# Gathered rows turned by VectorE in 32x32 blocks behind transfers inside SBUF, in place of TensorE transposes

## The chip, the cores and the metric

The kernel runs on one core of a Trainium2 chip. The metric is the device time of one execution in microseconds (us). Before the change the median of three executions was 1307.16 us (1306.89 to 1311.0); the profiled execution took 1307.46 us, of which 1305.5 us are the span that the trace covers. TensorE is PE in the profile, VectorE is DVE, ScalarE is ACT, GpSimd is POOL, SyncE is SP.

## What is computed

The input is an attention step over channels, followed by a layer of eight experts that choose their tokens by a sorted list.

```python
def _attn_ref(q, k, v, tau):                      # B, N, C = 4, 5056, 256
    qn = q / (np.linalg.norm(q, axis=1, keepdims=True) + 1e-06)
    kn = k / (np.linalg.norm(k, axis=1, keepdims=True) + 1e-06)
    s = kn.transpose(0, 2, 1) @ qn / tau
    a = np.exp(s - s.max(-1, keepdims=True))
    a /= a.sum(-1, keepdims=True) + 1e-09
    return v @ a                                  # x: 20224 tokens of 256

def _moe_ref(x, w_gate, w1, w2):                  # E, F = 8, 1024; cap = 2528
    order = np.argsort(-(x @ w_gate).flatten())
    # each token goes to the first expert in this order that still has room
    for e in range(E):
        mask = assigned == e
        out[mask] = np.maximum(x[mask] @ w1[e], 0.0) @ w2[e]
```

Every expert gets exactly 2528 tokens, that is 19 columns of 128 and one of 96 on a chip with 128 partitions.

## The kernel before, in words

**Stages.** To about 320 us the kernel computes the attention and writes its output x, row by row, to a table `x_d` in HBM. From there to the end it runs the experts one after another. Which tokens an expert gets is found while the expert ahead of it is computed: `route` and `compact` are generators whose steps are mixed into the work of the experts, most of them on VectorE, with small matmuls on TensorE (lines 585, 598, 794) and sums on ScalarE (line 851).

**Chunks.** An expert's 20 columns are cut in chunks: six in expert 0 (2, 4, 4, 4, 4, 2 columns) and five of four columns in the others. For every column `load_x` lets GpSimd gather 128 rows of `x_d` into `xg` (line 1088; two buffers), 256 numbers for each token. The matmuls need the rows turned, with the 256 numbers along the partitions. `turn` does that: for each half of the 256 (`kb`) and each column one PE transpose into a PSUM tile `ph` (line 1125), eight for a chunk of four columns; then ScalarE writes the high part `xH` (line 1131) and VectorE the rest `xL` (line 1134), because each product is computed as three products of a high and a low part.

**Layers.** `layer1` runs 8 blocks of 6 matmuls for a chunk (line 1162) into `ph`, four buffers that it shares with `turn`; ScalarE writes `hH` (line 1165), VectorE `hL` (line 1170). `layer2` runs 24 matmuls for each column into `py` (line 1194, two buffers); ScalarE copies the result to `y` (line 1199) and GpSimd scatters it to the output (line 1201). The order is layer1 of chunk c, then layer2 of chunk c-1. `turn` of chunk c+1 stands in layer2 of c-1 behind its first column, and asks for the gathers of the chunk two further on; `gather` then issues one of them behind each block or column (two for the first chunk of an expert). The first chunk of the next expert is turned in the last layer2 of an expert (`next_turn`), once its gathers are taken to have landed; its second one in the first layer1, at block 5.

**What sets the order.** The program writes the order of every engine out by hand. `Order` keeps two clocks, `o.pe` and `o.dve`, in estimated nanoseconds; `post` puts a VectorE step with a due time and a price into a line, `hook` runs the earliest of that line and of the routing steps, `flush` runs the line up to a tile. Each engine then executes its own instructions in the order written; they wait for each other by semaphores alone. The waits that the estimates stand for (`GATHER_LAT`, 7500) issue nothing.

Of the kernel before, what the change touches and what calls it, by code (L numbers as in the profile page):

```python
# [74 lines left out]
LAYER_LAT = 1050  # L75
SPLIT_LAT = 1600
LOAD_LAT = 8500
GATHER_LAT = 7500
START_TICKS = 27
EARLY_PRIO = 4  # L80
COMPACT_PRIO = 2
# [5 lines left out]
def attention_moe(ctx: ExitStack, tc: tile.TileContext, q, k, vt, tau, wg, w1t, w2t, tabs, out):  # L87
# [990 lines left out]
    def load_x(p, c, paced=False):  # L1078
        idx = routed[p]["src"]
        xg = ffx.tile([128, 4, C], F32, name="xg", bufs=2)  # L1080

        def fetch(i, col, n):
            at = idx[:n, col:col + 1]
            if paced:
                at = ffx.tile([128, 1], I32, name="pace", bufs=4)[:n]
                S.activation(at, idx[:n, col:col + 1], AF.Copy)
            P.memset(spacer, 0.0)
            P.indirect_dma_start(out=xg[:n, i, :], out_offset=None, in_=x_d,  # L1088
                                 in_offset=bass.IndirectOffsetOnAxis(ap=at, axis=0))
        for i, col in enumerate(cols_of(p, c)):  # L1090
            queue.append((p, c, lambda i=i, col=col, n=n_in(col): fetch(i, col, n)))
        xgs[p, c] = xg

# [3 lines left out]
                queue.pop(0)[2]()  # L1097

    queue = []
    unit = [0]  # L1100
    phs = []
    turned = [0]
# [9 lines left out]
    def turn(p, c):  # L1112
        while any(e[:2] == (p, c) for e in queue):
            gather()
        xg = xgs[p, c]
        nt = n_of(p, c)
        xH = ffx.tile([128, 2, 512], F32R, name="xH")
        xL = ffx.tile([128, 2, 512], F32R, name="xL")
        xts[p, c] = (xH, xL)
        pts = []  # L1120
        for kb in range(2):
            pt = ph_tile()
            for i, col in enumerate(cols_of(p, c)):
                n = n_in(col)
                PE.transpose(pt[:, i * 128:i * 128 + n].bitcast(F32R), xg[:n, i, kb * 128:(kb + 1) * 128].bitcast(F32R),  # L1125
                             identr[:n, :n])
            pts.append((kb, pt, unit[0]))
        o.pe += 440
        o.hook()
        for kb, pt, u in pts:  # L1130
            S.activation(xH[:, kb, 0:nt], pt[:, 0:nt], AF.Copy)  # L1131

            def low(kb=kb, pt=pt):
                V.tensor_tensor(xL[:, kb, 0:nt], pt[:, 0:nt], xH[:, kb, 0:nt].bitcast(F32), op=OP.subtract)  # L1134
            o.post(o.pe + TURN_LAT + (90 + nt) * kb, 90 + nt, low, u)
        turned[0] = unit[0]
        ahead = chunks.index((p, c)) + 2
        if ahead < len(chunks):
            p_, c_ = chunks[ahead]
            want(("idx", p_), lambda: load_x(p_, c_))  # L1140
# [68 lines left out]
    with tc.manual_schedule():  # L1209
# [60 lines left out]
        for p in range(E):  # L1270
# [3 lines left out]
            def turn_at(c):  # L1274
                return lambda: turn(p, c)

            turns = [] if last else [p + 1]

            def next_turn(force=False):
                if not turns:  # L1280
                    return
                if force:
                    o.until(("idx", p + 1))
                    settle()
                    while queue:
                        gather()
                    while o.pe < routed[p + 1]["time"] + GATHER_LAT:
                        o.tick(100)
                if done.get(("idx", p + 1)) and o.pe >= routed[p + 1]["time"] + GATHER_LAT:
                    turn(turns.pop(), 0)  # L1290

            if not last:
                want(("ei", p + 1), lambda p=p: load_w(p + 1))
# [5 lines left out]
                layer2(p, 0, h[0], {1: [turn_at(1)]})  # L1299
                h[1] = layer1(p, 1, {5: [turn_at(2)]})  # L1300
            else:
                h[0] = layer1(p, 0, {5: [turn_at(1)], **pieces})
            for c in range(1 if p else 2, nchunk):
                h[c] = layer1(p, c, {})
                ins = {}
# [9 lines left out]
                    ins = {min(1, cuts[p][c - 1] - 1): [w1]}  # L1315
                layer2(p, c - 1, h[c - 1], ins)
            layer2(p, nchunk - 1, h[nchunk - 1], {i: [next_turn] for i in range(1, 4)})
            while turns:
                next_turn(True)


# [61 lines left out]
```

## Time and profile before

| what | value |
| --- | --- |
| median of three executions | 1307.16 us |
| profiled execution | 1307.46 us |
| its span | 1305.5 us |
| PE busy | 1284.6 us, 98% |
| DVE busy | 795.4 us, 61% |
| ACT busy | 559.2 us, 43% |
| POOL busy | 378.3 us, 29% |
| PE transposes of gathered rows (line 1125) | 320 |
| gathers (line 1088) | 160 |

Busy time of PE is the time with a matmul in the array; matmuls overlap, so what a matmul costs is read from the distance between the starts of two that follow each other, not from its own duration. A row of the timeline or of the chain of waits starts with the start in us and the length in us. A row of the groups ends with busy us, mean ns of one instruction, and the idle time before them with what ended it. A row of stages holds busy us of each engine with the number of instructions, then the granted PE clock (1.00 is full), the share of the DMA engines and GB/s.

### The profile page before, as it was taken

To read this page: it belongs to the slowest core of one execution; us is meant where nothing else is said; L and a number is where in the kernel's file an instruction comes from. 1 tells how busy PE (TensorE), PEld (TensorE's weight loads), DVE (VectorE), ACT (ScalarE), POOL (GpSimd) and SP (SyncE) were. 2 spreads that over 40 slices of the span, in tenths; PEclk is the share of its full clock that TensorE was granted. 3 is DMA by queue.
4 is the path that set the end of the run, shared out by engine and by line. 5 is a ranking of instruction groups with operands and counts; after the bars stand their busy time and mean duration, and the time that the engine had idled before them with its cause. 6 is when DMAs were issued, how large, how long until landed. Compare 5 with 4: busy or idle time off the path is not lost.

```text
span 1305.5 us, 23749 instructions
## 1 busy us (share of the span) xinstructions
PE 1284.6 (98%) x9381; PEld 1151.9 (88%) x9381; DVE 795.4 (61%) x1973; ACT 559.2 (43%) x1249; POOL 378.3 (29%) x690
## 2 busy tenths in 40 slices
PE   7999999998999999999999999999999999999998
PEld 6879976997889988898899888988989998898998
DVE  6778695998778677768667767663343224334321
ACT  6547743565324344325335435335543234334321
POOL 1000000001522534333324433342342433334222
PEclk9989999999999999999999999999999999999999
DMA  8999874345202213112112211221131113111100
GB/s 298 337 399 387 296 273 157 141 164 190 73 24 86 66 40 105 53 43 104 47 35 77 78 40 37 73 84 34 46 116 36 56 46 109 45 41 56 36 29 32
DMA packets 42638, 143.18 MB, mean 110 GB/s; under 512 B 8224, under 2 KB 13216, under 8 KB 37920
## 3 DMA queue, kind: packets, MB, share of 16 engines
q0 software_dynamic: 17664, 58.22, 13.7%
q1 hardware_dynamic: 15328, 62.40, 13.2%
q10 hardware_dynamic: 9536, 21.06, 4.1%
q8 instruction: 73, 1.20, 0.4%
q14 instruction: 37, 0.30, 0.1%
HBM read 99.97 MB, written 41.68 MB: 109 GB/s over the span
## 4 chain that ended last, share of the span: by engine, by line
PE 86%; issue 5%; DVE 5%; POOL 2%; DMA 1%; ACT 1%; POOLq 0%; SPq 0%; DVEq 0%; ACTq 0%
PE ph L1162 32%; PE py L1194 31%; PE s L309 8%; PE px L258 8%; PE pc L585 3%; PE ph L1125 2%; POOL out_dram L1201 1%; PE px L413 1%; PE pi L794 1%; DVE acc_k L318 1%; DMA x_d<-xs 1%; DVE acc_q L318 1%; DVE ua L1064 1%; DVE yy L372 1%; DMA ua<-in_q_dram 1%
## 5 line engine op out<-in xcount | busy, mean ns | idle before, releaser
L1194 PE MATMUL py<-ua,hH 128*128 128x256 f32 (+1 forms) x2560 | 464.7, 282 | 0.0
L1162 PE MATMUL ph<-xH,ua 128*128 128x512 f32 (+3 forms) x1312 | 415.3, 391 | 0.3 <-ACT xH L1131 0.3
L1194 PEld LDWEIGHTS py<-ua,hH 128*128 128x128 f32 (+1 forms) x2560 | 391.8, 186 | 2.7 <-issue 0.2
L1170 DVE SCALAR_TENSOR_TENSOR hL<-ph,hH 128x512 fp32r<-128x512 f32 (+3 forms) x328 | 219.7, 671 | 231.9 <-ACT hH L1165 226.5
L1194 PE MATMUL py<-ua,hL 128*128 128x256 f32 (+1 forms) x1280 | 358.4, 280 | 0.0
L1201 POOL DMA_INDIRECT out_dram<-y,idx x160 | 160.9, 1005 | 519.3 <-ACT y L1199 471.9
L1165 ACT ACTIVATE hH<-ph 128x512 fp32r<-128x512 f32 (+3 forms) x328 | 191.1, 583 | 238.2 <-PE ph L1162 232.6
L1162 PEld LDWEIGHTS ph<-xH,ua 128*128 128x128 f32 x1312 | 244.2, 189 | 48.3 <-ACT xH L1131 0.4
L1162 PE MATMUL ph<-xL,ua 128*128 128x512 f32 (+3 forms) x656 | 256.0, 390 | 0.6 <-DVE xL L1134 0.6
L1194 PEld LDWEIGHTS py<-ua,hL 128*128 128x128 f32 (+1 forms) x1280 | 238.6, 186 | 0.0
L1199 ACT ACTIVATE y<-py 128x256 f32<-128x256 f32 (+1 forms) x160 | 61.5, 384 | 340.2 <-PE py L1194 281.9
L1088 POOL DMA_INDIRECT xg<-x_d,src x156 | 156.3, 1002 | 78.9 <-issue 33.6
L309 PE MATMUL s<-ua 128*128 128x256 f32 x640 | 146.9, 390 | 7.1 <-DMA ua<-in_q_dram 7.1
L309 PEld LDWEIGHTS s<-ua 128*128 128x128 f32 x640 | 124.3, 196 | 27.8 <-issue 6.7
L1162 PEld LDWEIGHTS ph<-xL,ua 128*128 128x128 f32 x656 | 124.2, 189 | 23.6 <-DVE xL L1134 0.7
L317 ACT ACTIVATE sq<-ua 128x1024 f32<-128x1024 f32 x72 | 75.1, 1054 | 42.2 <-DVE acc_k L318 14.3
L1134 DVE TENSOR_TENSOR xL<-ph,xH 128x512 fp32r<-128x512 f32 (+3 forms) x82 | 51.1, 665 | 56.1 <-ACT xH L1131 56.1
L261 ACT ACTIVATE xs<-px 128x512 f32<-128x512 f32 (+1 forms) x96 | 49.7, 527 | 52.0 <-PE px L258 50.7
L258 PE MATMUL px<-aH,vh 128*128 128x256 f32 (+1 forms) x216 | 62.8, 293 | 0.4 <-ACT aH L220 0.4
L851 ACT ACTIVATE junk<-pi,rhalf 128x160 bf16<-128x160 f32 x140 | 53.9, 391 | 18.7 <-PE pi L794 18.1
L258 PE MATMUL px<-aH,vl 128*128 128x256 f32 (+1 forms) x216 | 61.2, 284 | 0.0
L258 PE MATMUL px<-aL,vh 128*128 128x256 f32 (+1 forms) x216 | 61.1, 284 | 0.0
(291 smaller groups left out, 1321.6 us busy)
## 6 DMA issues: line engine op xcount, KB each, us to landing
x_d<-xs ACTq DMA_DIRECT2D x39, 512.0 KB, 2.8
ua<-in_k_dram SPq DMA_DIRECT2D x35, 512.0 KB, 6.2
ua<-in_q_dram SPq DMA_DIRECT2D x35, 512.0 KB, 7.2
vr<-in_vt_dram SPq DMA_DIRECT2D x14, 1024.0 KB, 9.7
ua<-in_vt_dram SPq DMA_DIRECT2D x4, 1024.0 KB, 4.9
out_dram<-y,idx POOLq DMA_INDIRECT x160, 2.4
xg<-x_d,src POOLq DMA_INDIRECT x156, 2.8
ub<-in_vt_dram SPq DMA_DIRECT2D x2, 1024.0 KB, 12.6
```

The costliest lines, as they stand in the source:

```text
L258: mm = PE.matmul(px[:, i * C:i * C + width], lhsT=l_, rhs=a_, start=(j == 0), stop=(j == len(terms) - 1))
L309: newest[0] = PE.matmul(sb[:, ib * C:(ib + 1) * C], lhsT=kt[:, t, ib * 128:(ib + 1) * 128], rhs=qt[:, t, :], start=(first and t == 0 and i ...
L317: S.activation(sq, t_, AF.Square)
L851: S.activation(junk, pi[:, i * W:i * W + COLS], AF.Sign, bias=rhalf[:, g0 + i:g0 + i + 1], scale=-1.0, accum_out=sgn[:, g0 + i:g0 + i + 1])
L1088: P.indirect_dma_start(out=xg[:n, i, :], out_offset=None, in_=x_d, in_offset=bass.IndirectOffsetOnAxis(ap=at, axis=0))
L1134: V.tensor_tensor(xL[:, kb, 0:nt], pt[:, 0:nt], xH[:, kb, 0:nt].bitcast(F32), op=OP.subtract)
L1162: PE.matmul(ph[:, 0:nt], lhsT=l[:, w], rhs=x_[:, kb, 0:nt], start=(i == 0), stop=(i == 5))
L1165: S.activation(hH[:, fb, 0:nt], ph[:, 0:nt], AF.Relu)
L1170: V.scalar_tensor_tensor(hL[:, fb, 0:nt], ph[:, 0:nt], 0.0, hH[:, fb, 0:nt].bitcast(F32), op0=OP.max, op1=OP.subtract)
L1194: PE.matmul(py[:n, 0:C], lhsT=l[:, fb, tk], rhs=w[:, d], start=(j == 0), stop=(j == 23))
L1199: S.activation(y[:n], py[:n, 0:C], AF.Copy)
L1201: sd = P.indirect_dma_start(out=out, out_offset=bass.IndirectOffsetOnAxis(ap=idx[:n, col:col + 1], axis=0), in_=y[:n], in_offset=None)
```

## The change

For all chunks but the first three of expert 0 (38 chunks, 150 columns) the PE transposes go. Behind the last gather of such a chunk, `exchange` issues 16 transfers on SP's queue, each from 32 partitions of `xg` to 32 partitions of a new tile `xq` (two buffers), 8 pieces of 32 numbers for each partition. They bring each 32x32 block to the partitions on which it ends. `turn` then posts two DVE transposes of 128x512, which turn all blocks in place and write the same PSUM tiles, with the ScalarE copy to `xH` behind each; the steps to `xL` follow. The second chunk of the next expert may now be turned in the last layer2 as well; where it isn't, it is turned in the first layer1 at block 2. What is taken as the time to landing counts from the last gather and its exchange (`LANDED_LAT`, 7500).

```diff
@@ -75,7 +75,9 @@
 LAYER_LAT = 1050
 SPLIT_LAT = 1600
 LOAD_LAT = 8500
-GATHER_LAT = 7500
+LANDED_LAT = 7500
+FIRST_BY_V = 3
+TURN_FB = 2
 START_TICKS = 27
 EARLY_PRIO = 4
 COMPACT_PRIO = 2
@@ -1078,6 +1080,20 @@
     def load_x(p, c, paced=False):
         idx = routed[p]["src"]
         xg = ffx.tile([128, 4, C], F32, name="xg", bufs=2)
+        cols = cols_of(p, c)
+        by_v = p > 0 or c >= FIRST_BY_V
+
+        def exchange():
+            back = chunks.index((p, c)) - 2
+            o.flush(turn_unit.get(chunks[back], 0))
+            xq = ffx.tile([128, 4, 8, 32], F32, name="xq", bufs=2)
+            xgs[p, c] = xq
+            parts = xg.rearrange("p i (k m) -> p (i k) m", k=2)
+            for g in range(4):
+                n = sum(n_in(col) > 32 * g for col in cols)
+                for j in range(4):
+                    nc.sync.dma_start(xq[32 * j:32 * j + 32, g, 0:2 * n],
+                                      parts[32 * g:32 * g + 32, 0:2 * n, 32 * j:32 * j + 32])
 
         def fetch(i, col, n):
             at = idx[:n, col:col + 1]
@@ -1087,7 +1103,11 @@
             P.memset(spacer, 0.0)
             P.indirect_dma_start(out=xg[:n, i, :], out_offset=None, in_=x_d,
                                  in_offset=bass.IndirectOffsetOnAxis(ap=at, axis=0))
-        for i, col in enumerate(cols_of(p, c)):
+            if i == len(cols) - 1:
+                if by_v:
+                    exchange()
+                landed[p, c] = o.pe + LANDED_LAT
+        for i, col in enumerate(cols):
             queue.append((p, c, lambda i=i, col=col, n=n_in(col): fetch(i, col, n)))
         xgs[p, c] = xg
 
@@ -1097,6 +1117,8 @@
                 queue.pop(0)[2]()
 
     queue = []
+    landed = {}
+    turn_unit = {}
     unit = [0]
     phs = []
     turned = [0]
@@ -1118,16 +1140,40 @@
         xL = ffx.tile([128, 2, 512], F32R, name="xL")
         xts[p, c] = (xH, xL)
         pts = []
-        for kb in range(2):
+        by_v = p > 0 or c >= FIRST_BY_V
+        src = xg
+        for kb in range(2) if by_v else ():
+            pt = ph_tile()
+            u = unit[0]
+            pts.append((pt, u))
+
+            def turn_v(kb=kb, pt=pt):
+                rows = xg.rearrange("p g (i k) a -> p k i g a", k=2)[:, kb]
+                turned_ = pt.rearrange("p (i g n) -> p i g n", i=4, g=4)
+                full = nt // 128
+                V.transpose(turned_[:, 0:full], rows[:, 0:full])
+                if nt % 128:
+                    V.transpose(turned_[:, full, 0:nt % 128 // 32], rows[:, full, 0:nt % 128 // 32])
+                S.activation(xH[:, kb, 0:nt], pt[:, 0:nt], AF.Copy)
+            o.post(o.pe, 130 + nt * 1.13, turn_v, pts[0][1])
+        for kb, (pt, u) in enumerate(pts):
+            def low_v(kb=kb, pt=pt):
+                V.tensor_tensor(xL[:, kb, 0:nt], pt[:, 0:nt], xH[:, kb, 0:nt].bitcast(F32), op=OP.subtract)
+            o.post(o.pe + 1400 + 650 * kb, 90 + nt, low_v, u)
+            turn_unit[p, c] = u
+        for kb in () if by_v else range(2):
             pt = ph_tile()
             for i, col in enumerate(cols_of(p, c)):
                 n = n_in(col)
                 PE.transpose(pt[:, i * 128:i * 128 + n].bitcast(F32R), xg[:n, i, kb * 128:(kb + 1) * 128].bitcast(F32R),
                              identr[:n, :n])
             pts.append((kb, pt, unit[0]))
-        o.pe += 440
-        o.hook()
-        for kb, pt, u in pts:
+        if by_v:
+            o.hook()
+        else:
+            o.pe += 440
+            o.hook()
+        for kb, pt, u in () if by_v else pts:
             S.activation(xH[:, kb, 0:nt], pt[:, 0:nt], AF.Copy)
 
             def low(kb=kb, pt=pt):
@@ -1274,7 +1320,7 @@
             def turn_at(c):
                 return lambda: turn(p, c)
 
-            turns = [] if last else [p + 1]
+            turns = [] if last else [(p + 1, 0), (p + 1, 1)]
 
             def next_turn(force=False):
                 if not turns:
@@ -1284,10 +1330,10 @@
                     settle()
                     while queue:
                         gather()
-                    while o.pe < routed[p + 1]["time"] + GATHER_LAT:
+                    while o.pe < landed[turns[0]]:
                         o.tick(100)
-                if done.get(("idx", p + 1)) and o.pe >= routed[p + 1]["time"] + GATHER_LAT:
-                    turn(turns.pop(), 0)
+                if o.pe >= landed.get(turns[0], 1e12):
+                    turn(*turns.pop(0))
 
             if not last:
                 want(("ei", p + 1), lambda p=p: load_w(p + 1))
@@ -1299,7 +1345,9 @@
                 layer2(p, 0, h[0], {1: [turn_at(1)]})
                 h[1] = layer1(p, 1, {5: [turn_at(2)]})
             else:
-                h[0] = layer1(p, 0, {5: [turn_at(1)], **pieces})
+                if (p, 1) not in xts:
+                    pieces[TURN_FB] = pieces.get(TURN_FB, []) + [turn_at(1)]
+                h[0] = layer1(p, 0, pieces)
             for c in range(1 if p else 2, nchunk):
                 h[c] = layer1(p, c, {})
                 ins = {}
@@ -1315,7 +1363,7 @@
                     ins = {min(1, cuts[p][c - 1] - 1): [w1]}
                 layer2(p, c - 1, h[c - 1], ins)
             layer2(p, nchunk - 1, h[nchunk - 1], {i: [next_turn] for i in range(1, 4)})
-            while turns:
+            while turns and turns[0][1] == 0:
                 next_turn(True)
```

The names in the orders below: `xg` and `xq` are a chunk's gathered and exchanged rows, `y` a finished column of layer2, `ph` and `py` PSUM tiles, `pc`, `Dm`, `Dr`, `Ex` and `ge` belong to routing. Numbers tell buffers of one name apart. Lines are those of each kernel's own file: the gather is line 1088 before and 1104 in the changed kernel, the scatter 1201 and 1247. Between the rows stand small memsets, which are left out.

**POOL, where expert 0 ends and expert 1 begins.** Before, from the scatter of the last column of the third chunk from the end on:

```order
L1201 DMA out_0_dram<-y_4752,idx_3148 20224x256
...
L1088 DMA xg_4877<-x_d_66,src_4843 128x256
...
L1201 DMA out_0_dram<-y_4931,idx_3148 20224x256
...
L1088 DMA xg_4878<-x_d_66,src_4843 128x256
...
L1201 DMA out_0_dram<-y_4997,idx_3148 20224x256
```

In the changed kernel, y_5063 being the last column of the next to last chunk, y_5138 and y_5186 the two columns of the last one:

```order
L1247 DMA out_0_dram<-y_5010,idx_3148 20224x256
...
L1104 DMA xg_5014<-x_d_66,src_4973 128x256
...
L1247 DMA out_0_dram<-y_5063,idx_3148 20224x256
...
L1104 DMA xg_5014<-x_d_66,src_4973 128x256
...
L1247 DMA out_0_dram<-y_5138,idx_3148 20224x256
...
L1104 DMA xg_5015<-x_d_66,src_4973 128x256
...
L1247 DMA out_0_dram<-y_5186,idx_3148 20224x256
...
L1104 DMA xg_5015<-x_d_66,src_4973 128x256
```

Expert 1's first chunk (xg_4877 before, xg_5014 now) had all four gathers ahead of the next to last chunk's layer2; now two stand ahead of the scatter of that chunk's last column and two behind it, and three of the second chunk's four (xg_5015) stand behind the expert's last scatter.

**DVE, at the same place.** Before, the steps to xL of expert 1's first chunk:

```order
L588 TENSOR_TENSOR Dm_5183<-pc_5140,dmask_132 128x8x6
L591 TENSOR_REDUCE Dr_5191<-Dm_5183 128x6
L594 TENSOR_TENSOR Ex_4491<-Dr_5191,jsel_129 120x16x6
L1134 TENSOR_TENSOR xL_5152<-ph_5153,xH_5151 128x512
L1134 TENSOR_TENSOR xL_5152<-ph_5158,xH_5151 128x512
L605 TENSOR_REDUCE mxs_5206<-pc_5140 128x15
```

In the changed kernel:

```order
L593 TENSOR_REDUCE Dr_5235<-Dm_5233 128x6
L1154 STREAM_TRANSPOSE ph_5239<-xq_5071 128x512
L1154 STREAM_TRANSPOSE ph_5240<-xq_5071 128x512
L1161 TENSOR_TENSOR xL_5238<-ph_5239,xH_5237 128x512
L1161 TENSOR_TENSOR xL_5238<-ph_5240,xH_5237 128x512
L1216 SCALAR_TENSOR_TENSOR hL_5249<-ph_5250,hH_5248 128x512
L1066 TENSOR_TENSOR ua_5261<-ub_4400,ua_5260 128x512
L1216 SCALAR_TENSOR_TENSOR hL_5249<-ph_5263,hH_5248 128x512
L1154 STREAM_TRANSPOSE ph_5275<-xq_5196 128x512
L1154 STREAM_TRANSPOSE ph_5276<-xq_5196 128x512
L1161 TENSOR_TENSOR xL_5274<-ph_5275,xH_5273 128x512
L1161 TENSOR_TENSOR xL_5274<-ph_5276,xH_5273 128x512
```

The turns of expert 1's first chunk (from xq_5071) and second chunk (from xq_5196) stand in DVE's line with only two blocks of layer1 (hL of ph_5250 and ph_5263) between them.

**ACT, in the last layer2 of expert 1** (changed kernel). y_6892 is the third column of that layer2, xH_6831 the first chunk of expert 2:

```order
L1245 ACTIVATE y_6825<-py_6797 128x256
L1157 ACTIVATE xH_6831<-ph_6833 128x512
L1157 ACTIVATE xH_6831<-ph_6834 128x512
L1245 ACTIVATE y_6892<-py_6838 128x256
L1245 ACTIVATE y_6953<-py_6915 96x256
```

and POOL at that place, xg_6624 being the second chunk of expert 2:

```order
L1247 DMA out_0_dram<-y_6825,idx_5028 20224x256
...
L1104 DMA xg_6624<-x_d_66,src_6546 128x256
...
L1247 DMA out_0_dram<-y_6892,idx_5028 20224x256
...
L1104 DMA xg_6624<-x_d_66,src_6546 128x256
...
L1247 DMA out_0_dram<-y_6953,idx_5028 20224x256
```

The copy of the third column to y now stands behind the two copies that need DVE's transposes, and the last gather of expert 2's second chunk stands behind that column's scatter.

**PE and DVE in that layer2's last column** (changed kernel): PE's matmul into pc_6808 stands behind eight of the column's 24 matmuls and reads Ex_6257, which DVE writes behind the two transposes of expert 2's first chunk.

```order
L1154 STREAM_TRANSPOSE ph_6833<-xq_6677 128x512
L1154 STREAM_TRANSPOSE ph_6834<-xq_6677 128x512
L1161 TENSOR_TENSOR xL_6832<-ph_6833,xH_6831 128x512
L590 TENSOR_TENSOR Dm_6872<-pc_6808,dmask_132 128x8x6
L1161 TENSOR_TENSOR xL_6832<-ph_6834,xH_6831 128x512
L593 TENSOR_REDUCE Dr_6883<-Dm_6872 128x6
L596 TENSOR_TENSOR Ex_6257<-Dr_6883,jsel_129 120x16x6
```

So that routing step has moved behind the turn.

## The prediction, made before the changed kernel was run

> **What bounds the kernel now.** I read the page's busy times and its chain first, then the stages, then the waits of PE from 320 us on.
>
> ```profile
> PE 1284.6 (98%) x9381; PEld 1151.9 (88%) x9381; DVE 795.4 (61%) x1973; ACT 559.2 (43%) x1249; POOL 378.3 (29%) x690
> PE 86%; issue 5%; DVE 5%; POOL 2%; DMA 1%; ACT 1%; POOLq 0%; SPq 0%; DVEq 0%; ACTq 0%
> 400.00:500.00 100.00, 99.40 (x838) 89.95 (x837) 78.53 (x222) 41.47 (x117) 44.48 (x75) 1.00 0.22 71
> 700.00:800.00 100.00, 100.00 (x822) 88.78 (x820) 71.61 (x215) 41.06 (x116) 39.55 (x71) 1.00 0.20 65
> 1000.00:1100.00 100.00, 100.00 (x664) 91.04 (x663) 35.23 (x53) 36.22 (x71) 35.77 (x66) 1.00 0.19 64
> PE ph L1125 <- DMA xg<-x_d,src: 1.1, 1, 1.1
> PE ph L1162 <- ACT xH L1131: 0.3, 1, 0.3
> ```
>
> PE sets the time: it is busy throughout the experts, and its waits there are five, of 1.1 us down to 0.3 us. So every PE instruction that goes is a gain, and every wait put in front of PE is a loss. DVE has a quarter of its time free while routing runs and two thirds later.
>
> **What goes.** The price of a turn on PE is the distance from the first transpose to the matmul behind it.
>
> ```profile
> L1125 PE MATMUL ph<-identr,xg x320: 213/247/283, 323.1 to 1260.1; 128*128 128x128 f32 x160
> 716.64 0.39 PE L1162 MATMUL ph<-xH,ua 128*128 128x512 f32 x1
> 716.87 0.80 PE L1125 MATMUL ph<-identr,xg 128*128 128x128 f32 x8
> 717.51 0.46 PE L1162 MATMUL ph<-xH,ua 128*128 128x512 f32 x1
> ```
>
> 716.87 to 717.51 is 0.64 us for eight, 80 ns each (0.247 us is the length of one, not the distance). 150 columns lose two transposes each: 300 x 0.08 = **24 us**, at most, since nothing is waited for around them.
>
> The Trainium skill ("TensorE: Matmul & The Clock Gate", Part 4) gives about 275 ns for a transpose in a kernel's context; the sum by that would be 82 us off. The trace disagrees with it here: back to back they start every 80 ns, so I take 24.
>
> **What comes on DVE and ACT.**
>
> ```profile
> L416 DVE STREAM_TRANSPOSE nf<-px 128x512 f32<-128x512 f32 x8 | 5.7, 717 | 5.7 <-PE px L413 5.7
> L1134 DVE TENSOR_TENSOR xL<-ph,xH 128x512 fp32r<-128x512 f32 x64 | 41.1, 684 | 46.1 <-ACT xH L1131 46.1
> 1099.69 1.08 ACT L1131 ACTIVATE xH<-ph 128x512 fp32r<-128x512 f32 x2
> 1131.38 11.20 PE ph L1162 x48
> 1096.49 2.83 PE py L1194 x24
> 545.24 0.51 PE pc L585 x20
> ```
>
> The nearest transpose goes from PSUM to SBUF, this one from SBUF to PSUM; I take the same 0.72 us. Two for a chunk are 1.44 us, over 37.5 chunks' worth 54 us, hidden in DVE's free time: a chunk lasts 11.2 us in layer1 and four columns of 2.8 us in layer2, so DVE rises by 6%, to 78 to 84% in the routing stages. From data landed to the first matmul of layer1 it takes 0.72 us (transpose), 0.54 (xH), and to the second 0.65 more (xL starts behind the second transpose): 2.25 us with the handoffs. In the steady order three columns, 8.5 us, lie between turn and layer1: covered.
>
> **What comes on SP.** Each exchange is 16 issues, the time to landing counts from the last.
>
> ```profile
> 2.13 0.43 SPq L299 DMA_DIRECT2D ua<-in_q_dram  x1
> 2.60 0.43 SPq L299 DMA_DIRECT2D ua<-in_k_dram  x1
> 7.81 0.33 SPq L299 DMA_DIRECT2D ua<-in_k_dram  x1
> 8.18 0.43 SPq L299 DMA_DIRECT2D ua<-in_q_dram  x1
> L304 SPq DMA_DIRECT2D ua<-in_q_dram x4: 589/596/602, 32.1 to 182.9; - x4
> ua<-in_k_dram SPq DMA_DIRECT2D x1, 128.0 KB, 2.3
> xg<-x_d,src POOLq DMA_INDIRECT x156, 2.8
> ```
>
> In a burst one issue follows another after 0.47 us (2.13 to 2.60); the shortest step is 0.37 (7.81 to 8.18), the longest for a small piece 0.60 + 0.05. A small transfer lands after 2.3 us, a gather after 2.8. So an exchange takes 15 x 0.47 + 2.3 = **9.4 us**, with bounds of 7.9 (15 x 0.37 + 2.3) and 12.5 (15 x 0.65 + 2.8). No transfer inside SBUF is in the trace; 9.4 is the burst that is most like it. In the steady order the last gather stands in layer1 of a chunk and its turn behind two layer1 and five columns, some 35 us: covered. From expert 3 on at least six columns of layer2, 17 us, lie between the last gather of a first or second chunk and its turn: just enough.
>
> **What is not covered: the starts of experts 1 and 2.** There routing ends late, and the orders above leave little between gathers and turn.
>
> ```profile
> 1087.22 0.95 POOL L1088 DMA_INDIRECT xg<-x_d,src  x1 [0.22 <-issue]
> 1088.48 0.95 POOL L1088 DMA_INDIRECT xg<-x_d,src  x1 [0.21 <-issue]
> 1100.07 0.99 POOL L1201 DMA_INDIRECT out_dram<-y,idx  x1 [8.07 <-ACT y L1199]
> ```
>
> *Expert 1.* Zero is the end of the column of y_5063. A scatter can start 0.75 us behind its column (1099.32 to 1100.07), and POOL's steps follow each other after 1.26 us (1087.22 to 1088.48). One scatter and two gathers of the column before (from -2.1) are in front, so this scatter starts at 1.75, the last gather at 4.3, and lands at 7.1. The exchange lands at 7.2 + 9.4 = 16.6, and layer1's second matmul runs at 18.9. PE has only two columns and two groups of 20 small matmuls until then (2 x 2.83 + 2 x 0.51 = 6.7, second matmul at 6.9): it waits **12.0 us**. The second chunk's gathers end behind the last scatter (12.1, landed 14.9); its exchange starts at 15.0, behind the first on SP, and lands at 24.4. Its transposes hold DVE, which holds hL, and `ph` has four buffers: block 4 of layer1 needs the buffer that the second chunk's first half sits in, so it starts at 24.4 + 2.3 = 26.7, while block 3 ends at 18.7 + 5.6 = 24.3: **2.4 us**. Together 14.4.
>
> ```profile
> 454.56 0.21 DVE L588 TENSOR_TENSOR Dm<-pc,dmask 128x48 f32<-128x48 f32 x1 [1.82 <-PE pc L585]
> 454.80 0.24 DVE L591 TENSOR_REDUCE Dr<-Dm 128x6 f32<-128x48 f32 x1
> 455.08 0.26 DVE L594 TENSOR_TENSOR Ex<-Dr,jsel 120x96 fp32r<-120x96 f32 x1
> ```
>
> *Expert 2.* Zero is the end of the column behind which the first chunk's last two gathers stand. Landing of the exchange again 16.6. PE has four columns, two groups and a third of a column (13.3 us) and then reads Ex, which stands behind both transposes, both xL and three small steps: 1.5 us to the first xL, 2 x 0.65 for both, 0.7 for the steps below and 0.1 for handoffs, 3.6 in all. PE goes on at 20.2, a wait of 6.9. ACT holds y_6892 behind xH (19.1), so POOL scatters at 19.4 and issues the second chunk's last gather at 20.7; landed 23.5, exchanged 33.0, block 4 at 35.3. Without waits block 4 would have started at 13.3 + 1.9 (rest of the column) + 5.6 (four blocks) + 0.5 (a group among them) = 21.3. Both waits together: **14.0**.
>
> The sum: 1307.5 (profiled execution) - 23.8 (37.5 turns of 0.635, between the 0.63 and 0.64 that turns take) + 14.4 + 14.0 = 1312.1. With the bounds of the exchange the two starts cost 12.9 + 11.1 and 20.2 + 20.3, so 1307.7 and 1324.2.
>
> **The clock** adds to it.
>
> ```profile
> 322.00:326.00 4.00, 2.08 (x10) 1.12 (x8) 3.93 (x4) 0.66 (x2) 0.66 (x2) 1.00 0.19 58
> 326.00:330.00 4.00, 3.84 (x19) 3.84 (x20) 1.51 (x5) 0.87 (x4) 1.03 (x2) 0.57 0.02 4
> 330.00:335.00 5.00, 5.00 (x60) 4.96 (x59) 3.89 (x11) 2.56 (x9) 3.10 (x6) 1.00 0.26 79
> ```
>
> After the half idle stretch at 322 the granted clock fell to 0.57 over 4 us: (1 - 0.57) x 4 = 1.7 us lost. The first wait at each start would lose this inside what the second wait then takes anyway; only the last wait (7 us, expert 2) adds it, at even odds 0.9. That makes **1313 us**, 6 above the median of 1307.16, to which the profiled execution is 0.3 us longer.
>
> The Trainium skill (same page, Part 1) says that the clock halves after an idle window of about 3.4 us and comes back after as long a busy one. The drop at 326 agrees; by that rule each long wait costs 1.7 us more and the sum is 1313, without it 1312.
>
> **Rivals.** *A, faster: the starts are hidden.* Should gathers at the starts run further ahead of PE than I laid out, or the 16 issues overlap so that an exchange takes 3 us, each start costs 4 us or less and 24 - 8 = 16 remain: 1291. For it: before, these starts had no wait; against it, 0.37 us is the shortest step in any burst on SP. *B, even: the lower bound.* An exchange of about 8 us gives 1308, all gain spent at two starts. For it speaks that 32 KB are less than any transfer in the burst rows. *C, much slower.* Either the upper bound (1324), or DVE becomes the bound while routing runs: some 22 of the turns ((900 - 326) / 23 us for a chunk, less the three that stay), 32 us of DVE work, fall before 900 us, where DVE is 72 to 79% busy and routing's steps hang on it; a third of that on PE is 10 us, 1323. Against it: no wait of PE in the list above was over 1.1 us. The point from which it decides is PE waiting for the routing matmuls in every expert. That the blocks wouldn't go where they should is no rival: both orders fill the same tiles.
>
> **How the numbers follow.** Forecast (1309 to 1320) 0.44, A 0.18, B 0.26, C 0.12. Its own range is 1308 to 1320; for 8 in 10, with A's end mostly inside and C's bound nearly, **1292 to 1323**. What can be told from no change is 0.3%, 3.9 us: faster is A and a little of B, 0.20; same, 1303.2 to 1311.1, is the rest of B and the lower edge of the forecast, 0.30; slower 0.50.
>
> **What would show it.** The gain: PE from layer2 to layer2 in a late expert 3.2 us shorter (five turns), no wait at any turn there. The cost: idle PE of about 12 us before expert 1's first layer1 and 7 us twice around expert 2's, put down to DVE transposes or xH, and the transposes there waiting for transfers. SP's 16 issues 0.47 us apart, landing 2.3 us later; transposes 0.72 us. Wrong would be: steps under 0.3 us on SP (A), waits of a few us at every expert's start (C), or late experts that aren't shorter.

## The result, and the profile after

| | before | after |
| --- | --- | --- |
| median | 1307.03 us (four executions beside the changed kernel's) | 1328.47 us (four, 1326.58 to 1329.27) |
| ratio after/before | | 1.0151, 95% interval 1.0135 to 1.0168 |
| profiled execution | 1307.46 us | 1329.27 us, span 1327.5 us |

The change makes the kernel 1.5% slower, 21 us. The forecast was 1313 us, with a range of 1292 to 1323: the direction was right, but the loss of 21 us is more than three times the 6 that were forecast, and the time lies above the range.

The page of the kernel after, busy time first, then the group of the new DVE transposes (busy us, mean ns, idle before and what ended it):

```profile
PE 1270.5 (96%) x9081; PEld 1132.6 (85%) x9081; DVE 845.0 (64%) x2065; ACT 561.2 (42%) x1249; POOL 381.1 (29%) x690
L1154 DVE STREAM_TRANSPOSE ph<-xq 128x512 f32<-128x512 f32 (+2 forms) x76 | 48.0, 667 | 46.0 <-DMA xq<-xg 45.1
```

PE is busy for 14 us less and the kernel is 22 us longer, so PE now idles some 36 us more. DVE idled 45 us for exchanges. The stages show where; a row holds the stretch, busy us of PE, PEld, DVE, ACT and POOL, then the granted clock.

```profile
400.00:500.00 100.00, 82.62 (x611) 73.19 (x610) 65.93 (x174) 36.62 (x105) 34.55 (x60) 0.90 0.33 81
600.00:700.00 100.00, 87.21 (x606) 75.87 (x607) 69.35 (x178) 38.44 (x100) 28.11 (x51) 0.91 0.32 74
1000.00:1100.00 100.00, 100.00 (x689) 91.38 (x688) 42.83 (x98) 42.80 (x121) 38.62 (x75) 1.00 0.36 83
```

Before, PE was busy for 99.4 us of 400 to 500. Now 17 are idle there, and the granted clock is 0.90; from 600 to 700 it is the same again. From 1000 to 1100 PE is busy throughout. The PE waits of the kernel after from 320 us on (us in total, times, longest) and PE's four long ones with the one at expert 3, in order of time (the bracket is the idle time before the row):

```profile
PE ph L1208 <- ACT xH L1157: 13.2, 1, 13.2
PE pc L600 <- DVE Ex L596: 11.9, 2, 9.4
PE ph L1208 <- DVE xL L1161: 11.7, 2, 7.7
...
468.67 0.80 PE L1208 MATMUL ph<-xH,ua 128*128 128x512 f32 x1 [13.15 <-ACT xH L1157]
480.14 0.80 PE L1208 MATMUL ph<-xH,ua 128*128 128x512 f32 x1 [3.96 <-DVE xL L1161]
604.89 0.45 PE L600 MATMUL pc<-Ex,ones_q 128*128 128x96 f32 x1 [9.35 <-DVE Ex L596]
622.75 0.79 PE L1208 MATMUL ph<-xH,ua 128*128 128x512 f32 x1 [7.70 <-DVE xL L1161]
742.97 0.30 PE L600 MATMUL pc<-Ex,ones_q 128*128 128x64 f32 x1 [2.60 <-DVE Ex L596]
```

Two waits stand at the start of expert 1, two at expert 2's, a small one at expert 3's. Each ends behind DVE transposes, and these wait for the exchange. At expert 1's start, from the timelines of POOL, SP and DVE (start, length), with the row of SP's issues (min/median/max ns):

```profile
452.52 0.95 POOL L1104 DMA_INDIRECT xg<-x_d,src  x1 [0.22 <-issue]
455.48 10.40 SPq L1095 DMA_DIRECT2D xq<-xg  x16
467.26 1.32 DVE L1154 STREAM_TRANSPOSE ph<-xq 128x512 f32<-128x512 f32 x2 [11.23 <-DMA xq<-xg]
478.00 1.32 DVE L1154 STREAM_TRANSPOSE ph<-xq 128x512 f32<-128x512 f32 x2 [3.26 <-DMA xq<-xg]
L1095 SPq DMA_DIRECT2D xq<-xg x608: 585/609/1787, 354.4 to 1262.8; - x152
```

The last gather is issued at 452.5 and has landed by 455.5, where SP starts; the exchange takes until 467.3, 11.8 us. Its 16 issues take 10.4 us. Without the 0.61 of the last one that is 9.8 us for 15 steps, 0.65 each, and 2.0 remain from the start of the last issue to the landing. Last, the stretches of work behind the four long waits (the granted clock is the third number from the end):

```profile
468.60:472.00 3.40, 3.33 (x7) 2.43 (x8) 1.29 (x2) 0.67 (x3) 2.75 (x7) 0.51 0.64 123
480.10:485.60 5.50, 5.46 (x13) 4.30 (x14) 3.69 (x6) 1.35 (x3) 3.09 (x6) 0.50 0.72 145
604.80:608.50 3.70, 3.61 (x17) 3.61 (x18) 2.40 (x9) 0.00 (x0) 1.44 (x4) 0.50 0.22 71
622.70:629.00 6.30, 6.25 (x15) 4.90 (x16) 3.79 (x7) 3.09 (x7) 3.13 (x6) 0.50 0.66 135
```

PE works 18.9 us at half the clock, which is 9.4 us lost (half of each stretch). Now the books close: 1307.5 - 23.8 (the gain as forecast) + 34.2 (four waits) + 9.4 + 2.6 (expert 3) = 1329.9, beside 1329.3.

### The profile page after: what moved, and what is told of

Same layout as the page of the kernel before. It is cut to its first block, busy times and chain, and to the rows that moved or that the text cites. A ratio compares the mean times of both kernels' runs of the same rounds, so it can differ in the third digit from the quotient of the medians.

```text
span 1327.5 us, 24172 instructions
## 1 busy us (share of the span) xinstructions
PE 1270.5 (96%) x9081; PEld 1132.6 (85%) x9081; DVE 845.0 (64%) x2065; ACT 561.2 (42%) x1249; POOL 381.1 (29%) x690
## 3 DMA queue, kind: packets, MB, share of 16 engines
q0 software_dynamic: 17664, 58.22, 13.7%
## 5 line engine op out<-in xcount | busy, mean ns | idle before, releaser
L1208 PEld LDWEIGHTS ph<-xH,ua 128*128 128x128 f32 x1312 | 247.4, 192 | 75.2 <-ACT xH L1157 13.3
L1208 PE MATMUL ph<-xL,ua 128*128 128x512 f32 (+3 forms) x656 | 259.2, 395 | 0.6 <-DVE xL L1180 0.6
L1154 DVE STREAM_TRANSPOSE ph<-xq 128x512 f32<-128x512 f32 (+2 forms) x76 | 48.0, 667 | 46.0 <-DMA xq<-xg 45.1
L1161 DVE TENSOR_TENSOR xL<-ph,xH 128x512 fp32r<-128x512 f32 (+2 forms) x76 | 48.8, 672 | 30.9 <-ACT xH L1157 29.1
L1157 ACT ACTIVATE xH<-ph 128x512 fp32r<-128x512 f32 (+2 forms) x76 | 42.7, 588 | 59.0 <-DVE ph L1154 53.4
```

Of the source, the lines that this page charges most:

```text
L1208: PE.matmul(ph[:, 0:nt], lhsT=l[:, w], rhs=x_[:, kb, 0:nt], start=(i == 0), stop=(i == 5))
```

## The experiments

The kernels ran in five series, each on one chip with the kernel before beside them: 1308.3 us (first), 1336.6 (second), 1307.4 (third), 1334.4 (fourth), 1307.7 (fifth). In the second and fourth the kernel before took some 28 us longer; they are told at their place, and ratios are taken within a series. The changed kernel ran in none of the five but beside 1307.0 us, so a comparison with it goes across series.

### The exchange by itself

**The DVE transposes without the exchange.**

```diff
-            xq = ffx.tile([128, 4, 8, 32], F32, name="xq", bufs=2)
-            xgs[p, c] = xq
...
-                    nc.sync.dma_start(xq[32 * j:32 * j + 32, g, 0:2 * n],
-                                      parts[32 * g:32 * g + 32, 0:2 * n, 32 * j:32 * j + 32])
...
-                rows = xg.rearrange("p g (i k) a -> p k i g a", k=2)[:, kb]
+                rows = xg.rearrange("p i (k g a) -> p k i g a", k=2, g=4)[:, kb]
```

> All transfers of the exchange are left out; the DVE transposes read the gathered rows themselves, so the blocks stand in the wrong order. Theory (the loss is the landing of the exchange, 11.8 us behind that of the gathers, at the starts of experts 1 and 2): the waits of 13.2 and 4.0 us at expert 1 shrink to under 3 us together, those of 9.4 and 7.7 us at expert 2 and of 2.6 us at expert 3 go, and with them the drops of the granted clock behind them; the gain of 23.8 us shows whole: 1284 to 1289 us. Rival (the DVE transposes, their place in DVE's order and the handoffs cost the time): the waits stay at more than half, 1305 or more.

Measured: 1286.4 us, ratio 0.9839 (0.9808 to 0.987). Its PE waits that the kernel before doesn't have, from 320 us on:

```profile
PE ph L1201 <- DVE xL L1154: 2.8, 3, 2.0
PE ph L1201 <- ACT xH L1150: 1.9, 1, 1.9
```

As the theory had it: 21.9 us are gained, so DVE's transposes, their handoffs and their place in DVE's order cost at most the 2 us that are missing from 23.8. Gathers and scatters stand in the same order in this kernel and the changed one, so the difference between them, 42 us, hangs on the exchange.

**The exchange without the DVE transposes** (`by_v = False` in `turn`, transfers still issued).

> All exchanges are issued, but nothing reads their result: the turns stay on PE as in the kernel before. Theory (the exchange costs only where somebody waits for its landing): within 3 us of the kernel before, 1304 to 1310 us. Rival (the pieces of 128 bytes, 38 x 1024 rows of them each way, hold up gathers, scatters or weights on the DMA engines): 1313 us or more, with PE waits for gathers or weights.

Measured: 1305.27 us, ratio 0.9982 (0.9959 to 1.0006). 608 transfers of small pieces disturb neither gathers nor scatters enough to be seen. So it is not their traffic, it is the waiting for their landing.

**Twice the issues, half the size.**

```diff
-                    nc.sync.dma_start(xq[32 * j:32 * j + 32, g, 0:2 * n],
+                    for a, z in ((0, n), (n, 2 * n)):
+                        nc.sync.dma_start(xq[32 * j:32 * j + 32, g, a:z],
```

> Each of the 16 transfers of an exchange is cut in two: 32 issues of half the size. Theory (an issue has a fixed price of 0.65 us, and 16 of them make up most of the 11.8 us): an exchange takes 10 us longer, each of the two starts about 21 us longer, since the second chunk's exchange stands behind the first on SP, and the starts from expert 3 on, with some 17 us between gather and turn, wait too: over 1370 us, issues still 0.6 us apart. Rival (the price goes by the pieces or bytes of an issue): issues 0.33 us apart, time as with 16, 1328 us.

Measured: 1439.77 us (one execution). SP's issues and the largest PE waits of this kernel:

```profile
L1096 SPq DMA_DIRECT2D xq<-xg x1216: 585/599/1881, 349.7 to 1389.2; - x174
PE pc L600 <- DVE Ex L596: 38.2, 2, 19.5
PE ph L1209 <- DVE xL L1162: 33.9, 4, 17.5
PE py L1241 <- ACT y L1246: 27.7, 4, 11.6
PE ph L1209 <- ACT xH L1158: 22.6, 1, 22.6
```

Half the size has nearly the same median, 599 beside 609 ns. Between 8 and 4 pieces for each partition the price is one of the issue, not of its bytes or pieces, and every exchange pays it 16 times.

**DVE from expert 3 on** (`by_v = p >= 3`).

> Only experts 3 to 7 are turned by DVE; all before them by PE. Theory: 25 turns at 0.635 us are gained, 15.9 us, less up to 3 us at the start of expert 3 where PE waited 2.6 us: 1291 to 1294 us. Rival (DVE is the bound while routing runs, or the steady order waits too): gain below 8 us, 1299 or more.

Measured: 1294.46 us, ratio 0.9895 (0.9861 to 0.9929). 13.9 us below the kernel before of its series; PE waits at Ex for 2.9 us in two pieces, 2.3 of them at 865.6 us and so not at expert 3's start, which lies near 740. The upper end of the forecast is missed by half a us.

### The starts: a prediction that fell

**The two starts by PE, and by DVE alone.** The predicate `by_v` leaves out the chunks (1,0), (1,1), (2,0), (2,1), or holds for these alone; `turn` of a PE chunk stands where it stood before the change. A third kernel leaves out (3,0) and (3,1) as well.

> As changed, but the first two chunks of experts 1 and 2 are turned by PE, as in the kernel before. Theory (the whole loss sits at these two starts, 21.9 and 22.4 us, with 2.4 to 3 us more at expert 3): 33.5 turns at 0.635 us are gained, 21.3 us, less about 3 us at expert 3: 1287 to 1290 us. Rival (a good part of the loss is spread over the steady order, DVE in the routing stages above all): 1300 us or more.

> The same with the first two chunks of expert 3 by PE too. Theory: two turns more stay, 1.3 us, and the wait of 2.6 us at expert 3 goes: 1285 to 1289 us, 0.5 to 2 us below the kernel with two starts by PE. Rival (the wait at expert 3 has another cause than the exchange): 1.3 us above it.

> Only the first two chunks of experts 1 and 2 are turned by DVE behind the exchange, all others by PE. Theory: the two losses stand alone, 21.9 + 22.4 us less the 2.5 us of four turns: 1307 + 41.8 = 1349 us, 1344 to 1353. Rival (the loss is spread over all chunks): under 1325.

Measured (second series, before 1336.57 us): ratios 0.9952 (0.9932 to 0.9971), 1.0012 (0.9997 to 1.0027) and 1.0028 (1.0013 to 1.0044). None was as the theory had it; the first and the third came out as their rivals had it. But the chip differed in something that the records show. The same group of DVE, in the kernel with the unused exchange (first series) and in the one with only the starts by DVE (second):

```profile
L1215 DVE SCALAR_TENSOR_TENSOR hL<-ph,hH 128x512 fp32r<-128x512 f32 (+3 forms) x328 | 219.5, 670 | 218.9 <-ACT hH L1210 214.2
L1219 DVE SCALAR_TENSOR_TENSOR hL<-ph,hH 128x512 fp32r<-128x512 f32 (+3 forms) x328 | 218.7, 670 | 239.4 <-ACT hH L1214 145.8 <-issue 81.3 <-ACT junk L853 9.6
```

The instructions take the same 670 ns, but DVE stood 81 us ahead of them with nothing to wait for. So the three were run again.

> The first two chunks of experts 1 and 2 by PE again, all later ones by DVE. In the runs ahead of this one (kernel before 1336.6 us) DVE stood 60 to 80 us with nothing to wait for in the records, in all four kernels, where it stood 0 to 9 us in the others (kernel before 1308.3), so gains and losses of PE could not be read. Theory, where DVE does not stand so: 1287 to 1290 us, ratio 0.985 to 0.987. Rival (a part of the loss is spread over the steady order): ratio 0.995 or more here too.

> The same with the first two chunks of expert 3 by PE too. Theory: 0.5 to 2 us below the kernel with two starts by PE. Rival (the wait at expert 3 has another cause): 1.3 us above it.

> Only the first two chunks of experts 1 and 2 by DVE. Theory: 1344 to 1353 us beside 1307, ratio 1.028 to 1.035. Rival (the loss is spread over all chunks): ratio under 1.015.

Measured (third series, before 1307.44 us), where DVE did not stand so:

| kernel | us | ratio |
| --- | --- | --- |
| starts of experts 1, 2 by PE | 1292.32 | 0.9878 (0.9857 to 0.9899) |
| those of expert 3 too | 1298.02 | 0.9918 (0.9898 to 0.9938) |
| only the starts by DVE | 1314.34 | 1.0060 (1.0040 to 1.0080) |

The first does the whole work, is the fastest kernel that does so, and stands 36 us below the changed one, though 2 us short of what was expected. The second was expected below it and is 6 above: the order moved, and PE waited 6.0 us for `ext` of routing in three places instead of 2.3 in one; that is 3.7 of the 5.7 us, the rest is open. The third breaks the theory: the same four chunks behind the same exchange cost 7 us, not 42. That is the rival's figure, but not a loss spread over all chunks, since the first kernel turns all other chunks by DVE and gains. Where the difference lies is in POOL's rows: the last gather of expert 1's first chunk and PE's first matmul of expert 1, for the kernel before, and for the one with only the starts by DVE:

```profile
441.19 1.08 POOL L1088 DMA_INDIRECT xg<-x_d,src  x1 [0.23 <-issue]
457.29 0.39 PE L1162 MATMUL ph<-xH,ua 128*128 128x512 f32 x1
```

```profile
438.25 1.08 POOL L1107 DMA_INDIRECT xg<-x_d,src  x1 [0.22 <-issue]
441.34 23.64 SPq L1098 DMA_DIRECT2D xq<-xg  x32
456.07 0.51 PE L1211 MATMUL ph<-xH,ua 128*128 128x512 f32 x1 [2.23 <-ACT xH L1160]
468.61 0.79 PE L1211 MATMUL ph<-xH,ua 128*128 128x512 f32 x1 [4.60 <-DVE xL L1164]
```

There the gathers end 16 to 18 us ahead of expert 1. In the changed kernel the last one is issued at 452.52, and the last matmul of expert 0's layer2 follows at 454.15:

```profile
454.15 0.28 PE L1240 MATMUL py<-ua,hL 128*96 128x256 f32 x1
```

That is less than 2 us ahead. The order did it. Each DVE turn is booked with about 1.4 us more than the old one, the routing steps on DVE come later by that, and in the order the first chunk's last gather stands four columns later at expert 1 and six at expert 2. By themselves gathers that late cost little: the kernel without the exchange has them at the same places as the changed one, and no wait of PE there is longer than 2.0 us. The kernel with the starts by PE has those of expert 1 at the same place and waits 0.6 us for them.

### Late gathers

The new theory: the loss needs both, the 11.8 us of the exchange and the gathers that the turns' price moved behind.

**Nothing booked for the turns.**

```diff
-            o.post(o.pe, 130 + nt * 1.13, turn_v, pts[0][1])
+            o.post(o.pe, 0, turn_v, pts[0][1])
-            o.post(o.pe + 1400 + 650 * kb, 90 + nt, low_v, u)
+            o.post(o.pe + 1400 + 650 * kb, 0, low_v, u)
```

> All chunks by DVE as changed, but the order books 0 ns for the turn's four DVE steps, so that it keeps routing's steps early. The scatters between the first chunk's last gather and the end of the expert ahead go from 2 to 5 (expert 1) and 5 to 11 (expert 2); before the change they were 6 and 11. Theory (the loss needs both, the 11.8 us of the exchange and gathers that the order has put 4 to 6 columns later): expert 1 loses about 10 us as in the kernel with only the starts by DVE, experts 2 and 3 nothing: 1307 - 23.8 + 10 = 1293, 1289 to 1298 us. Rival (DVE really lacks the time, so booking it elsewhere only moves the wait): 1310 or more.

> The same, and the first two chunks of expert 1 by PE. Theory: no start loses anything, 35.5 turns at 0.635 us are gained, 22.5 us: 1283 to 1287 us. Rival (DVE lacks the time): 1300 or more.

> Only expert 0 keeps its turns on PE; its prices in the order stay. The first chunk's gathers of expert 1 then stand 6 columns ahead of the end, as before the change, those of expert 2 8 columns. Theory (late gathers and exchange together): expert 1 loses about 10 instead of 22 us, expert 2 under 4 instead of 22: 35 turns, 22.2 us, are gained: 1293 to 1299 us. Rival (the exchange alone at these two starts): 1328 or more.

> DVE turns the last three chunks of expert 0 and the first two of expert 1, PE all others; the gathers of expert 1's first chunk stand 2 columns ahead of the end, as in the changed kernel. Theory: expert 1's start loses 22 us as in the changed kernel, beside 10 with the gathers 6 columns ahead; 1307 - 2.9 + 22 = 1326, 1322 to 1329 us. Rival (the loss needs the turns of all chunks): 1314, as with only the starts by DVE.

Measured (fourth series, before 1334.37 us; DVE stood without a shown reason again, 74.4 us ahead of hL alone in the first): ratios 1.0000 (0.9984 to 1.0016), 0.995 (0.993 to 0.9969), 1.0017 (0.9997 to 1.0038) and 1.0087 (1.0066 to 1.0107). The order of the four is the one expected, the sizes are not: the second met its rival's figure, the others lie between theory and rival. The last stands 0.6% above the kernel with only the starts by DVE in the second series, 8 us where the theory had 12. It waits 8.7 us for `xH` ahead of expert 1 and 4.9 for `xL` at block 4. The third, with expert 0's turns on PE and the gathers four columns earlier, has no such wait for `xH`, but one of 8.9 us for `xL` at block 4. But these two series can't price it. The first two were run again.

> All chunks by DVE, gathers 5 and 11 scatters ahead of the end as in the order with 0 ns booked. In the runs ahead of this one (kernel before 1334.4 us) DVE again stood 58 to 91 us with nothing to wait for in the records. Theory, where it does not stand so: 1289 to 1298 us beside 1307, ratio 0.986 to 0.993; PE waits 4 to 8 us at expert 1, nothing over 1 us at expert 2. Rival (DVE lacks the time): ratio 1.000 or more.

> The same, and the first two chunks of expert 1 by PE. Theory: 1283 to 1287 us beside 1307, ratio 0.981 to 0.985. Rival (DVE lacks the time): ratio 0.990 or more.

Measured (fifth series, before 1307.73 us; DVE ran as in the first): 1313.66 us, ratio 1.0036 (1.0017 to 1.0055), and 1297.8 us, ratio 0.9926 (0.9906 to 0.9946). PE's waits of the first, in order of time at the start of expert 1, then in total from 500 to 1000 us:

```profile
462.13 0.79 PE L1208 MATMUL ph<-xH,ua 128*128 128x512 f32 x1 [4.26 <-ACT xH L1157]
475.58 0.80 PE L1208 MATMUL ph<-xH,ua 128*128 128x512 f32 x1 [3.47 <-DVE xL L1161]
...
PE pc L600 <- DVE Ex L596: 5.3, 3, 2.9
PE pc L778 <- DVE cb L772: 1.9, 1, 1.9
PE pc L587 <- DVE ge L618: 1.3, 2, 0.8
PE pc L706 <- DVE tb L703: 1.1, 1, 1.1
```

By their times both kernels came out as the rival had it (1.000 or more, 0.990 or more). By the waits the theory is half right. Every exchange is still there, and the waits at expert 1 fell from 17.1 to 7.7 us, those of 9.4 and 7.7 at expert 2 are gone, and with them 15 of the 21 us. At expert 1's start the four combinations now stand side by side, as the sum of PE's two waits there: early gathers without an exchange (before) none, late gathers without it 3.9 us, early gathers with it 6.8 (only the starts by DVE) or 7.7, late gathers with it 17.1. But the rival has its part: PE now waits some 10 us for small steps of routing in experts 2 to 4 (Ex, cb, ge, tb). The DVE time is real; what the order doesn't book, PE waits for in part. Of the 20 us by which 1313.66 stands above the 1293 of the theory, these waits are some 10. Half clock behind the waits at 475.6 and 755.2 us, for 6.1 and 6.4 us of work, is another 6; the rest is open. The kernel that books the time and keeps the two starts on PE is faster, 0.9878.

### The clock

**Matmuls that no one reads in three of the waits.**

```diff
+    WARM = {(1, 0, 0): 42, (1, 0, 4): 10, (2, 0, 4): 26}
+    def warm_py(key):
+        if key not in warm_t:
+            warm_t[key] = ps_2.tile([128, 512], F32, name="py")
+        PE.matmul(warm_t[key].rearrange("p (a c) -> p a c", a=4), lhsT=identr,
+                  rhs=identr[:, None, :].to_broadcast([128, 4, 128]), start=True, stop=True)
         for fb in range(8):
+            for _ in range(WARM.get((p, c, fb), 0)):
+                warm_py((p, c, fb))
```

> As changed, with matmuls that no one reads put into three of the four waits: 42 (9.1 us at full clock) ahead of expert 1's first block, 10 (2.2 us) and 26 (5.6 us) ahead of block 4 of the first layer1 of experts 1 and 2. The waits themselves stay. Theory (some 8 us of the loss is work at half the granted clock behind the waits, 6 of them behind these three): 1321 to 1324 us, and the granted clock stays at 1.00 in expert 1's start. Rival (the time behind the waits is lost by the waits alone): 1328 us, or more.

> Matmuls that no one reads in three of the four waits, 78 in all. Theory (some 6 us behind these three waits are work at half the granted clock): 1321 to 1324 us, ratio 1.010 to 1.013 beside 1.0151 without them, and the granted clock at 1.00 behind them. Rival: ratio 1.015 or more.

Measured: ratio 1.0112 (1.0091 to 1.0134) in the second series, 1324.58 us and 1.0116 (1.0087 to 1.0144) in the third. In the third, the stretches behind expert 1's two waits and expert 2's two:

```profile
467.20:475.60 8.40, 8.38 (x24) 6.38 (x25) 3.27 (x5) 3.39 (x6) 3.56 (x8) 0.66 0.56 111
479.60:485.00 5.40, 5.36 (x23) 4.19 (x24) 4.61 (x8) 3.07 (x6) 3.10 (x6) 1.00 0.71 146
602.60:606.20 3.60, 3.45 (x16) 3.45 (x17) 2.46 (x9) 0.00 (x0) 1.51 (x4) 0.52 0.23 73
618.00:626.00 8.00, 6.50 (x29) 4.79 (x28) 7.07 (x12) 5.39 (x10) 4.20 (x8) 1.00 0.59 116
```

Behind both second waits the clock stays full (0.50 without), and there the changed kernel lost 5.9 us (half of 5.5 and 6.3). The time fell by 0.35% of the kernel before, 4.6 us, which is near the 5.9, though the two intervals overlap by 0.1% and the two kernels ran in different series. Both results stay below the 1.015 of the rival. Ahead of expert 1 the 42 matmuls ended 3.45 us too early and the clock fell all the same: 0.66. Little hangs on that stretch, since the second wait ends when the second exchange lands.

## Why the prediction was wrong in size

- **The gain, 23.8 us: right.** Expert 6, whose routing is long over, shows it alone. First matmul of experts 6 and 7, before, then after:

```profile
1073.22 0.39 PE L1162 MATMUL ph<-xH,ua 128*128 128x512 f32 x1
1187.50 0.39 PE L1162 MATMUL ph<-xH,ua 128*128 128x512 f32 x1
```

```profile
1100.29 0.39 PE L1208 MATMUL ph<-xH,ua 128*128 128x512 f32 x1
1212.02 0.39 PE L1208 MATMUL ph<-xH,ua 128*128 128x512 f32 x1
```

114.28 us became 111.73: 2.55 less beside the 3.2 forecast, and 0.6 of the difference is a single wait for `y`. Without the exchange the whole kernel gained 21.9. The 80 ns from one PE transpose to the next were the right price. The Trainium skill ("TensorE: Matmul & The Clock Gate", Part 4) gives about 275 ns for a transpose in a kernel's context; taken as the price, that is an estimate of 82 us for the kernel without the exchange. It is the duration of one, and the trace does not disagree with it, as the prediction had it: one lasts 247 ns here.

- **The places and the mechanism: right.** Waits at the starts of experts 1 and 2, in the order named (xH, then xL at block 4; Ex, then xL), and transposes there waiting for transfers. Transposes take 0.67 us (0.72 forecast).

- **The price of an issue: the first step that failed.** "In a burst one issue follows another after 0.47 us" was read from transfers of another shape. These take 0.65, which stood there as the upper bound, from the row of issues of 0.60 us. The exchange takes 11.8 us (15 x 0.65 + 2.0) instead of 9.4. The prediction's own slope (40.5 - 28.4 = 12.1 us for the step from 9.4 to 12.5, with both starts) makes of these 2.4 us 9.4 more at the two starts. Measured there: 34.2 us of waits, and 3.6 us of half clock (of the stretches at 468.6 and 604.8) that lie ahead of second waits and would be waited for anyway, 37.8 against 28.4.

- **The clock: the second.** The prediction put 0.9 us, a loss of 1.7 for one wait at even odds. Behind the second waits alone it is 5.9. That the drop behind a first wait is swallowed by the second was right; that a drop costs 1.7 us each time was wrong (5.5 and 6.3 us of work at half clock cost 2.8 and 3.2), and that only one of the second waits would have one too.

- **Expert 3: the third.** "Just enough" was 2.6 us short. The second chunk's exchange stands behind the first one on SP there: the two take from 715.6 to 739.9 us, where its transposes start, 22 us behind the issue of its last gather (717.7), and Ex stands behind them on DVE. The sum of the three: 9.4 + 5.0 + 2.6 = 17.0, and 1329.3 - 1313.0 = 16.3.

- **Rivals.** C, much slower, is what came: its upper exchange bound gave 1324 without the clock. Its other half, DVE as the bound while routing runs, was put aside because PE's waits before were short. It did not show in the kernel after as waits for routing in every expert, but as late gathers: the order turned the DVE time into distance. The prediction counted the gathers at their new places without asking why they stood there. With nothing booked 15 of the 21 us go, and DVE's lack of time comes back as waits when it is hidden from the order.

- **The range** ended at 1323, though its upper bound of the exchange alone gave 1324.2 and the clock came on top. Even with the 1.7 us of a drop added it would have ended at 1325.9, below the 1328.47 measured: the rest of what the clock took, and expert 3, were missing from it.

## What to carry to other kernels

Price a burst of small transfers by the issue: count the issues, take the longest step in the trace for a new shape, and ask at each place how far ahead the last one can be started. Work that moves to an engine with free time isn't free where that engine's line also decides when something else is ready; look for what comes later in the order, not only for what the engine does in time. Where a change gains everywhere and loses at a few places, keep the old way at these: here that turned 21 us of loss into 15 of gain.

## What the runs showed of the hardware that was not expected

- On SP an issue of 32 x 8 x 32 numbers inside SBUF takes 0.61 us, and half of it 0.60: halving the transfer halves nothing.
- Waits shorter than expected halve the clock. In the kernel with nothing booked, one of 2.9 us is followed by 6.4 us of work at 0.50; with only the starts by DVE, one of 2.23 us (at 456.07, above) by 3.4 us. The 2.6 us at expert 3 in the kernel after had no drop. The rows are, in this order, of these three kernels:

```profile
755.20 0.42 PE L600 MATMUL pc<-Ex,ones_q 128*128 128x64 f32 x1 [2.94 <-DVE Ex L596]
751.34:754.75 3.41, 0.91 (x8) 0.71 (x7) 1.26 (x3) 0.50 (x1) 0.21 (x2) 1.00 0.44 85
754.75:758.16 3.41, 2.96 (x14) 2.97 (x15) 3.31 (x12) 1.07 (x3) 0.00 (x0) 0.50 0.35 51
```

```profile
453.25:456.66 3.41, 1.10 (x7) 0.55 (x5) 1.93 (x4) 1.24 (x3) 0.00 (x0) 1.00 0.31 53
456.66:460.07 3.41, 3.27 (x8) 2.65 (x9) 2.63 (x11) 0.73 (x3) 2.48 (x5) 0.50 0.44 80
```

```profile
738.20:741.61 3.41, 2.18 (x20) 1.95 (x18) 1.68 (x3) 0.98 (x2) 0.63 (x2) 1.00 0.33 76
741.61:745.03 3.42, 2.06 (x14) 1.89 (x15) 2.93 (x11) 0.86 (x3) 2.19 (x5) 1.00 0.11 38
```

In these traces the granted clock changes only at the ends of steps of 3.41 us: in the kernel after it is 0.50 for 13.7, 6.8, 10.2 and 10.2 us around the four waits, that is 4, 2, 3 and 3 steps. So it matters where a wait falls. The 2.23 us lie whole in one step, and so do 2.5 of the 2.94 us; PE is busy for 1.10 and 0.91 of 3.41 us there, and the next step is at half clock. The 2.6 us are split over two steps with 2.18 and 2.06 us busy, and nothing follows. Where between these the border lies is not sharp: in the kernel with the starts of expert 3 by PE too, a step with 2.20 us busy (455.24 to 458.65) was followed by half clock.

The Trainium skill ("TensorE: Matmul & The Clock Gate", Part 1) says that the clock halves after an idle window of about 3.4 us and comes back after a busy one. The return agrees (3.4 to 6.3 us of work at half clock, one window or two). The drop does not need a window that is idle throughout: steps with 0.91 and 1.10 us of work were enough, and the drop at 326 in the kernel before, which the prediction called in agreement, followed one with 1.33 us of work (322.75 to 326.16).

- In two of five series DVE stood 56 to 88 us ahead of `hL` with nothing to wait for in the records, in every kernel that was profiled there, its instructions as long as ever, and the kernel before, of which there is no trace from there, took 2% longer. What held DVE is open. There the gains by DVE turns shrank: 0.9952 beside 0.9878 for the same kernel.
